# A spectral filter and a two-layer perceptron on one core: the scheduler at build time replaced by a written order, tiles turned by DMA, bias added in place

## The chip, the core and the metric

The kernel runs on one core of a Trainium2 chip. The core has five instruction streams: TensorE (PE; its weight loads are PEld), VectorE (DVE), ScalarE (ACT), GpSimd (POOL) and SyncE (SP, which only issues transfers and waits). Each works through its own list in order, and semaphores order one against another. The metric is device microseconds of one execution, the median of several runs.

## What is computed

All arrays are bf16. `x` has 2048 rows of 640. Each row is normalized, and three terms are added:

```
def reference(A_x, A_w_r, A_w_i, B_x, B_w1, B_b1, B_w2, B_b2):
    x = A_x
    xn = _layernorm(x, axis=-1)
    return x + _A_ref(xn, A_w_r, A_w_i) + _B_ref(xn, B_w1, B_b1, B_w2, B_b2)
```

`_A_ref` is a two-dimensional real FFT, a product with a complex filter of 2048 x 321, and the inverse. `_B_ref` is `gelu(xn @ w1 + b1) @ w2 + b2` with w1 of 640 x 1536 and w2 of 1536 x 640.

## The kernel before

The 2048 rows are 16 tiles of 128. Work goes through these stages.

- *Loads.* SyncE issues the tiles of x, the weights, tables of cosines and sines, the bias row spread over the partitions (`b2bc`, L529), and the filter in 34 loads (`load_w`, L534; 17 real, 17 imaginary). The first third of the first weights goes out on ScalarE's queue (L514).
- *Normalization.* VectorE takes the statistics of a tile in two halves (L568, L570, L572), GpSimd raises the variance to -1/2 (L573), VectorE normalizes (L591).
- *Transposed tile for the perceptron.* TensorE turns each normalized tile in five products with an identity (L608, weights and products), and VectorE or ScalarE copies them out of PSUM into `xnT` (L481, L480).
- *Spectral, forward.* VectorE folds each pair of normalized tiles in six instructions (L620, L624), TensorE multiplies them with the table `gtab` (products "G"), the result goes to `XV`. Then the width stage forward (`etab`, six groups), small 32 x 32 products (`mtab`), the product with the filter on VectorE (L725, L729), small inverse products (`ntab`), copies to U, and sixteen transposing transfers of U to `XV`, issued by SyncE (L750). The width stage back (`getab`, six groups) reads all sixteen.
- *Perceptron.* First layer in blocks of 1, 1, 2, 2, 2, 4 and 4 tiles with 12 column chunks each, gelu on ScalarE (L658). Second layer tile by tile, in pieces of three chunks; each chunk is a pair of products of 512 and 128 columns. For the eight tiles of `KEEP` it is done early and kept.
- *End of a tile.* VectorE unfolds the width stage's result (L775, L780), TensorE multiplies it with `htab` on top of the second layer, VectorE adds the rest (L837), and SyncE stores the tile.
- *The rest, x + b2.* A 32-bit tile is set to the bias row (ScalarE, L805) or to the kept second layer plus the bias row (VectorE, L826); then GpSimd issues a transfer that adds the tile of x from HBM to it (L828), sixteen in all. This is the only use of accumulating transfers.

The order of every engine's list comes from a list scheduler that runs at build time: `Sched.schedule` (L194) takes the estimated cost of every operation (`mm_us`, `dve_us`, `act_us`), its priority (`PRIO`), gates such as `CHAIN`, and a due time for the filter (`WLATE`, L384), and places what can start first. `sync` (L293) then derives the semaphore waits. A buffer from a `Pool` is reused only when its earlier users are done; the normalized pair, `xn`, has two.

Of the kernel before, what the change touches and what calls it, by code (L numbers as in the profile page):

```python
# [7 lines left out]
BF = dt.bfloat16  # L8
# [5 lines left out]
D = 640  # L14
# [13 lines left out]
def _tables():  # L28
# [5 lines left out]
    for s2 in range(16):  # L34
        for m1 in range(64):
            qq, lo, n = m1 // 32, m1 // 16 % 2, m1 % 16
            pair, hi = n % 8 // 2 * 2 + n // 8, n % 2
# [44 lines left out]
    T["I"] = np.eye(128)  # L82
# [3 lines left out]
SWITCH = 0.095  # L86
HOLD = 0.1


def mm_us(n):  # L90
    return max(n / 2400.0 + 0.0027, 0.0265)


def dve_us(n, rate=1.0):
    return 0.066 + n / 960.0 / rate


def act_us(n, ptr=0):
    return 0.067 + n / 1200.0 + 0.078 * ptr


def pool_us(n):
    return 0.075 + n / 500.0


class Buf:
    def __init__(self, name, pool=None, size=1, zone=None):
        self.name, self.pool, self.size = name, pool, size
        self.zone = zone
        self.writers, self.readers = [], []  # L110
        self.slot = None
        self.prev = []
        self.left = None


class Pool:
    def __init__(self, n):
        self.free = [0.0] * n
        self.users = [[] for _ in range(n)]
        self.busy = [False] * n  # L120

    def find(self, buf, now):
        size, n = buf.size, len(self.free)
        best = None
        for lo, hi in buf.zone or [(0, n)]:
            for i in range(lo, hi - size + 1, size if size != 3 else 1):
                if any(self.busy[i:i + size]):
                    continue
                t = max(self.free[i:i + size])
                key = (max(t, now), sum(not b for b in self.busy[i & ~1:(i & ~1) + 2]), sum(not b for b in self.busy[i & ~3:(i & ~3) + 4]), t)  # L130
                if best is None or key < best[0]:
                    best = (key, t, i)
            if best is not None and best[1] <= now + 0.05:
                break
        return best and best[1:]

    def take(self, buf, i):
        buf.slot = i
        buf.prev = [u for j in range(i, i + buf.size) for u in self.users[j]]
        for j in range(i, i + buf.size):  # L140
            self.busy[j] = True

    def give(self, buf, t):
        for j in range(buf.slot, buf.slot + buf.size):
            self.busy[j] = False
            self.free[j] = t
            self.users[j] = buf.writers + buf.readers
# [6 lines left out]
LAT = {"pe": 0.2, "dve": 0.125, "act": 0.16, "pool": 0.12}  # L154


class Sched:
    def __init__(self, nc, engines):
        self.nc = nc
        self.ops = []  # L160
        self.engines = engines
        self.order = {e: [] for e in engines}

    def op(self, engs, prio, emit, reads=(), writes=(), after=(), nbytes=0, gate=(), rate=330e3, alts=None, late=0.0):
        o = Op()
        o.name = writes[0].name if writes else ""
        o.engs, o.prio, o.emit = engs, prio, emit
        o.reads, o.writes, o.after, o.gate = list(reads), list(writes), list(after), list(gate)
        o.nbytes, o.rate, o.late = nbytes, rate, late
        o.alts, o.alt = alts, None  # L170
        o.seq = len(self.ops)
        o.eng, o.done, o.inc, o.count, o.sem = None, False, False, None, None
# [8 lines left out]
    def cost(self, o, e):  # L181
        if o.alts is None:
            return dict(o.engs)[e], None, self.mode
        best = None
        for k, segs in enumerate(o.alts):
            m, t = self.mode, 0.0
            for mode, us in segs:
                t += us + (SWITCH if mode != m else 0.0)
                m = mode
            if best is None or t < best[0] - 1e-9:  # L190
                best = (t, k, m)
        return best

    def schedule(self):  # L194
        free = {e: 0.75 for e in self.engines}
        dma_free = 0.0
        self.mode = "128"
        pend = {e: [] for e in self.engines}
        for o in self.ops:
            for b in o.reads + o.writes:  # L200
                if b.pool is not None and b.left is None:
                    b.left = len(b.readers) + len(b.writers)
        waiting = {}
        users = {}
        for o in self.ops:
            pre = set(o.deps) | set(o.gate)
            waiting[o] = len(pre)
            for d in pre:
                users.setdefault(d, []).append(o)

        def avail(o):
            o.ready = max([o.late] + [d.end for d in o.deps] + [d.start for d in o.gate])
            for e, _ in o.engs:
                pend[e].append(o)
        for o in self.ops:
            if not waiting[o]:
                avail(o)
        left = len(self.ops)
        while left:
            best = None  # L220
            for e in self.engines:
                cands = []
                for o in pend[e]:
                    if o.done:
                        continue
                    r = o.ready
                    ok = True
                    held = []
                    for b in o.writes:
                        if b.pool is not None and b.slot is None:  # L230
                            f = b.pool.find(b, max(r, free[e]))
                            if f is None:
                                ok = False
                                break
                            r = max(r, f[0])
                            held += [(b.pool, i) for i in range(f[1], f[1] + b.size)]
                            for p, i in held[-b.size:]:
                                p.busy[i] = True
                    for p, i in held:
                        p.busy[i] = False  # L240
                    t = max(r, free[e])
                    if ok and len(o.engs) > 1:
                        mine = (t + dict(o.engs)[e], self.engines.index(e))
                        ok = all(e2 == e or (max(r, free[e2]) + d2, self.engines.index(e2)) > mine for e2, d2 in o.engs)
                    if ok:
                        cands.append((t, o))
                if not cands:
                    continue
                t0 = min(c[0] for c in cands)
                near = [c for c in cands if c[0] <= t0 + 0.03]  # L250
                if e == "pe" and self.mode != "128":
                    near = [c for c in cands if c[0] <= t0 + HOLD and c[1].alts and c[1].alts[0][0][0] == self.mode] or near
                t, o = min(near, key=lambda c: (-c[1].prio, c[1].seq))
                if best is None or t < best[0]:
                    best = (t, e, o)
            if best is None:
                raise RuntimeError("nothing can be scheduled: " + str([(e, [p.name for p in pend[e] if not p.done][:5]) for e in self.engines]))
            t, e, o = best
            if e == "pe":
                dur, o.alt, self.mode = self.cost(o, e)  # L260
            else:
                dur = dict(o.engs)[e]
            o.eng, o.start = e, t
            o.done = True
            pend[e] = [p for p in pend[e] if not p.done]
            free[e] = t + dur
            if o.nbytes:
                if e == "pool" and o.prio < 400:
                    o.end = t + 5.0
                else:  # L270
                    s = max(t + 1.1, dma_free)
                    dma_free = s + o.nbytes / o.rate
                    o.end = dma_free + 0.9
            else:
                o.end = t + dur + LAT[e]
            for b in o.writes:
                if b.pool is not None and b.slot is None:
                    b.pool.take(b, b.pool.find(b, t)[1])
# [595 lines left out]
```

## Time and profile before

| | us |
|---|---|
| runs | 157.84, 159.59, 160.26 |
| median | 159.59 |
| span of the profiled execution | 158.2 |
| TensorE busy | 148.9 |
| VectorE busy | 115.0 |
| ScalarE busy | 79.9 |
| GpSimd busy | 26.4 |

The profiled execution is known by its span, from the first to the last instruction; the median of the runs is 1.4 us above it. The span is read in stretches: 0 to 7 us, loads and the first normalization; to 51 us, normalization, transposes, first transform and first layers; to 106 us, filter stages between blocks of the perceptron; to 118 us, the last transposing transfers; to 158 us, width stage back, second layers and stores. A busy TensorE is not TensorE at its pace, since the durations of its products overlap; the pace is the distance from one start to the next.

### The profile page before, as it was taken

The numbers are of one execution on the slowest core, as the hardware profiler recorded it, in microseconds if no ns is written. First come the engines' busy times: TensorE is split into PE (matmuls) and PEld (weight loads), VectorE is DVE, ScalarE is ACT, GpSimd is POOL, SyncE is SP. The second block draws the span as 40 slices with busy tenths as digits, with TensorE's granted clock in tenths as the row PEclk, the third lists the DMA queues.
The fourth block names the chain that finished last, engine by engine and source line by source line (L and its number), as shares of the span: only waits on it lengthen the run. The fifth ranks groups of instructions, "written<-read, shape, count | busy, mean of one in ns | idle before, by whom it ended". The sixth has DMA issues, their size and how long they took to land.

```text
span 158.2 us, 4332 instructions
## 1 busy us (share of the span) xinstructions
PE 148.9 (94%) x1845; PEld 97.1 (61%) x1845; DVE 115.0 (73%) x251; ACT 79.9 (51%) x145; POOL 26.4 (17%) x33
## 2 busy tenths in 40 slices
PE   7699999999999999999999999999749899999993
PEld 7599899989766545445644444454336565665563
DVE  1689999999996448969676969913207999998222
ACT  3178989798984646638563564742402550220000
POOL 1112113233241302000920020022540000000000
PEclk9999999999999999999999999999978999999999
DMA  5999999979853504000799155386992204122111
GB/s 146 358 412 401 395 375 189 206 147 174 147 91 83 77 10 84 3 6 16 125 186 178 41 110 101 55 172 108 156 228 35 83 4 178 73 87 83 41 66 58
DMA packets 30410, 21.71 MB, mean 137 GB/s; under 512 B 12728, under 2 KB 28216, under 8 KB 30392
## 3 DMA queue, kind: packets, MB, share of 16 engines
q1 hardware_dynamic: 23336, 15.71, 37.8%
q0 software_dynamic: 6400, 5.24, 20.4%
q10 hardware_dynamic: 656, 0.49, 0.9%
q8 instruction: 14, 0.23, 0.6%
q14 instruction: 4, 0.03, 0.1%
HBM read 13.58 MB, written 2.62 MB: 102 GB/s over the span
## 4 chain that ended last, share of the span: by engine, by line
PE 80%; DMA 6%; DVE 5%; SPq 3%; ACT 3%; issue 1%; DVEq 0%; POOL 0%
PE ps L469 77%; DMA XV<-U 3%; SPq L750 3%; PE ps L608 3%; DMA X<-in_A_x_dram 2%; DVE T L725 2%; ACT Wf L480 1%; ACT XV L480 1%; DVE Xb L481 1%; DVE Wf L481 1%; DVE Z L729 1%; SPq L464 1%; ACT T L480 0%; DVEq L354 0%; POOL rstd L573 0%
## 5 line engine op out<-in xcount | busy, mean ns | idle before, releaser
L469 PE MATMUL ps<-W,gT 128*128 128x512 bf16 (+3 forms) x396 | 58.6, 298 | 0.5 <-DVE X L826 0.5
L469 PE MATMUL ps<-xnT,W 128*128 128x256 bf16 (+2 forms) x420 | 57.0, 288 | 0.2 <-ACT gT L658 0.2
L469 PEld LDWEIGHTS ps<-W,gT 128*128 128x128 bf16 x396 | 30.4, 99 | 25.1 <-issue 3.2
L658 ACT ACTIVATE gT<-ps,b1col 128x256 bf16<-128x256 f32 (+2 forms) x84 | 39.2, 504 | 10.8 <-PE ps L469 9.5
L469 PEld LDWEIGHTS ps<-xnT,W 128*128 128x128 bf16 x420 | 34.6, 98 | 15.3 <-issue 1.7
L480 ACT ACTIVATE Wf<-ps 128x960 bf16<-128x960 f32 (+1 forms) x9 | 7.6, 880 | 21.1 <-PE ps L469 21.1
L568 DVE BATCH_NORM_STATS2 stats<-X 128x6 f32<-128x320 bf16 x32 | 14.9, 474 | 3.4 <-DMA X<-in_A_x_dram 3.4
L828 POOL DMA_DIRECT2D xnT<-in_A_x_dram x8 | 12.9, 1694 | 24.2 <-ACT xnT L805 20.6
L828 POOL DMA_DIRECT2D X<-in_A_x_dram x8 | 7.4, 923 | 38.4 <-DVE X L826 36.3
L725 DVE TENSOR_TENSOR T<-Y,Wf 128x1288 bf16<-128x1288 bf16 x16 | 12.5, 822 | 0.6 <-issue 0.6
L469 PE MATMUL ps<-getab,XV 32*128 32x160 bf16 (+1 forms) x128 | 8.2, 253 | 3.2 <-DMA XV<-U 2.5
L573 POOL TENSOR_TENSOR rstd<-ve,mhalf 128x2 f32<-128x2 f32 (+1 forms) x9 | 6.4, 716 | 27.1 <-DVE ve L572 27.1
L481 DVE CAST Y<-ps 128x644 bf16<-128x644 f32 x8 | 6.6, 825 | 5.4 <-PE ps L469 5.4
L837 DVE TENSOR_TENSOR W<-ps,xnT 128x640 bf16<-128x640 f32 x8 | 6.5, 819 | 5.6 <-PE ps L469 5.4
L480 ACT ACTIVATE Xb<-ps 128x960 bf16<-128x960 f32 (+1 forms) x6 | 6.8, 1135 | 6.7 <-PE ps L469 6.7
L469 PEld LDWEIGHTS ps<-getab,XV 32*128 32x128 bf16 (+1 forms) x128 | 6.8, 147 | 5.0 <-DMA XV<-U 2.9
L481 DVE CAST Xb<-ps 128x960 bf16<-128x960 f32 (+1 forms) x6 | 6.7, 1122 | 4.2 <-PE ps L469 4.2
L480 ACT ACTIVATE Y<-ps 128x644 bf16<-128x644 f32 x8 | 5.6, 706 | 8.1 <-PE ps L469 8.1
L480 ACT ACTIVATE XV<-ps 128x1280 bf16<-128x1280 f32 (+1 forms) x7 | 8.0, 1145 | 3.4 <-PE ps L469 3.4
L826 DVE TENSOR_TENSOR X<-ps,b2bc 128x640 f32<-128x640 f32 x7 | 5.7, 818 | 4.8 <-PE ps L469 4.8
L624 DVE TENSOR_TENSOR T<-T 128x512 bf16<-128x512 bf16 (+1 forms) x32 | 8.7, 316 | 0.0
L608 PE MATMUL ps<-ident,T 128*128 128x128 bf16 x80 | 7.1, 220 | 1.3 <-DVE T L591 1.3
(46 smaller groups left out, 142.1 us busy)
## 6 DMA issues: line engine op xcount, KB each, us to landing
xnT<-in_A_x_dram POOLq DMA_DIRECT2D x8, 320.0 KB, 5.6
X<-in_A_x_dram POOLq DMA_DIRECT2D x8, 320.0 KB, 4.5
out_dram<-W SPq DMA_DIRECT2D x15, 160.0 KB, 1.8
X<-in_A_x_dram SPq DMA_DIRECT2D x7, 320.0 KB, 9.0
W<-in_B_w_dram SPq DMA_DIRECT2D x2, 960.0 KB, 12.9
Wf<-in_A_w_r_dram SPq DMA_DIRECT2D x15, 80.2 KB, 7.2
Wf<-in_A_w_i_dram SPq DMA_DIRECT2D x15, 80.2 KB, 3.8
W<-in_B_w_dram SPq DMA_DIRECT2D x1, 800.0 KB, 7.3
```

The source lines that it names most:

```text
L469: ins = e.matmul(o_, lhsT=lw, rhs=rh, start=st, stop=sp_, skip_group_check=True)
L480: return e.activation(dst(), src(), ACT.Copy, scale=scale)
L481: return e.tensor_copy(dst(), src())
L568: st_ops.append(K.op([("dve", 0.393)], pr, lambda e, _, c=c, h=h: e.bn_stats(stats[:, c, 6 * h:6 * h + 6], view(X, c * D + H2 * h, [[1, H2 ...
L573: K.op([("pool", 0.65)], pr, lambda e, _, a=a, b=b: e.tensor_tensor(out=rstd[:, a:b], in0=ve[:, a:b], in1=mhalf[:, a:b], op=ALU.pow), read ...
L608: ins = e.transpose(psb(tps.slot, [[1, 512]]).bitcast(BF)[:, 128 * j:128 * j + 128], xnv(n, 128 * j, [[1, 128]]), ident[:])
L624: ring_ops.append(K.op([("dve", dve_us(4 * w, 2))], pr, lambda e, _, op=op, x1v=x1v, xfv=xfv, o_=o_, o0=o0, o1=o1, w=w: e.tensor_tensor(ou ...
L658: K.op([("act", act_us(128 * nt, 1))], pr + PRIO["gelu"], lambda e, _, c0=c0, nt=nt, fc=fc, hps=hps: e.activation(gT[:, fc, 128 * c0:128 * ...
L725: filt_ops.append(K.op([("dve", dve_us(4 * KP, 2))], pr, lambda e, _, k=k, Y=Y, TB=TB, pair=pair: e.tensor_tensor(out=view(TT, TB.slot * 8 ...
L826: kept_ops.append(K.op([("dve", dve_us(D))], 30, lambda e, _, kps=kps, xov=xov, shaped=shaped: e.tensor_tensor(out=xov(0, D), in0=shaped(p ...
L828: K.op([("pool", 1.5)], 51, lambda e, _, c=c, xov=xov, shaped=shaped: e.dma_start(xov(0, D), shaped(xv[:, c, :]), accum_op=ALU.add), reads ...
L837: K.op([("dve", dve_us(w))], 95, lambda e, _, os_=os_, fps=fps, o0=o0, w=w, xov=xov, shaped=shaped, base=base: e.tensor_tensor(out=shaped( ...
```

## The change

`Sched`, its costs, priorities and gates are gone. `Plan` takes the order of all 775 operations and the place of every pooled buffer from two strings, `ORDER` and `SLOTS`, and derives the waits as before. One line of `ORDER` holds operations of several engines; each engine takes its own in the order in which they stand. Beside the order, the work itself is changed in these places:

- Tiles 4 to 15 are turned by a transposing transfer from SyncE (`td`); tiles 0 to 3 stay on TensorE (`tp`, copies `tc`).
- The bias row is added to x in SBUF, in bf16, by four accumulating transfers of four tiles each (`xs0`, `xs4`, `xs8`, `xs12`), issued by GpSimd after the normalizations of those tiles. The 32-bit tiles set on ScalarE and the sixteen transfers of x go. The early sum of a kept tile (`kk`) adds its second layer to x + b2; the last addition (`os`) of the other tiles reads x + b2.
- The filter comes in 18 loads of up to 16 x 16 rows that share a semaphore; the rows of the first transform's table are placed to suit.
- The identity is made on GpSimd. The first weights are loaded on SyncE's queue behind four tiles of x; only the bias of the first layer stays on ScalarE's.
- Weights of the second layer, tables and filter are issued after the last x has landed.
- The two halves of the second weights are waited for separately.
- The block ends without a GpSimd drain, and SyncE waits for the stores behind the block.

```diff
+BYDMA = tuple(range(4, 16))
+SUMS = [(c, c + 4) for c in range(0, 16, 4)]
...
+        for a, b in SUMS:
+            bs = K.buf(f"xs{a}")
+            K.op(f"xs{a}", "pool", lambda e, _, a=a, b=b: e.dma_start(
+                view(X, a * D, [[D, b - a], [1, D]]), view(b2bc, 0, [[0, b - a], [1, D]]), accum_op=ALU.add),
+                reads=[B_b2b] + B_x[a:b], writes=[bs], after=norm_ops[a:b], dma=f"xs{a}")
...
+                    K.op(f"kk{c}", "dve", lambda e, _, kps=kps, c=c, home=home: e.tensor_tensor(
+                        out=home, in0=shaped(psb(kps.slot, [[1, D]])), in1=shaped(view(X, D * c, [[1, D]])), op=ALU.add),
...
-                K.op([("pool", 1.5)], 51, lambda e, _, c=c, xov=xov, shaped=shaped: e.dma_start(xov(0, D), shaped(xv[:, c, :]), accum_op=ALU.add),
-                     reads=[xb2], writes=[xo], nbytes=327680, rate=150e3)
...
         for ri, wsrc in enumerate((A_w_r, A_w_i)):
...
+            for b in range(4):
+                off = ri * KP
+                load_w(f"W{ri}{b}p", wsrc, 32 * b, off, 16 * b, 16, 1)
+                if b:
+                    load_w(f"W{ri}{b}n", wsrc, 32 * b + 1, off, 128 - 16 * b, 16, -1)
+                else:
+                    load_w(f"W{ri}{b}m", wsrc, 1, off, 64, 1, 1)
+                    load_w(f"W{ri}{b}n", wsrc, 1, off + 2 * KP, 127, 15, -1)
...
-        block = es.enter_context(nc.Block())
+        with nc.Block(no_gpsimd_drain=True) as block:
...
+        for o in last:
+            nc.sync.wait_ge(o.sem, o.count)
```

Three places of `ORDER`: the start, the loads and transposes between tile 11 and the end of SyncE's early list, and the last inverse product (`d3.1`) up to the first group of the width stage back (`e0`). `h1.0.3` is block 1, chunk 0, second part of the first layer; `k` and `l` are second-layer pieces, `ge` a gelu, `W..` a filter load, `vt` a transposing transfer of U, `st`, `ag`, `ve`, `rs`, `nm` the normalization's steps, `f1`, `f2` the folds, `G` the first transform, `b` the width stage forward, `m` the product with the filter.

```
act:bias1 pool:id0 dve:warm0 sp:x0 pool:mhalf pool:xbpad1 pool:id1 pe:idle0 act:table sp:x2 sp:x1 sp:w1_0 sp:w1_1 sp:w1_2 dve:st0.1 sp:x4 dve:st0.0
sp:g pe:b1mm dve:ag0 act:b1cp dve:ve0 dve:st2.1 pool:rs0 dve:st1.1 sp:x6 dve:st1.0 pool:xbpad0 dve:nm0 sp:x14 dve:ag1 dve:st2.0 pe:tp0.3 sp:x12
pe:tp0.0 pe:idle1 act:tc0.3 dve:ve1 dve:st3.0 sp:x10 pool:rs1 dve:tc0.0 sp:x8 dve:st3.1 pe:h0.2.0 pe:h0.1.0 dve:nm1 pe:h0.4.0 dve:ag3 pe:h0.4.3
...
pool:xs8 sp:td11 dve:f15.1 dve:f15.0 pe:G8 dve:kk1 pe:G9 pe:k2.9 act:gx4.0 dve:f25.10 dve:f25.00 pe:h3.1.0 sp:td10 dve:f25.11 pe:h3.0.0 dve:f25.01
...
pe:h4.2.0 dve:f27.10 pe:h4.7.0 pe:h4.2.3 pe:G14 act:ge4.2 pe:h4.7.3 sp:i pe:G15 act:ge4.7 pe:h4.8.0 sp:W12p dve:gx7.2 act:gx7.0 pe:h4.8.3 pe:h4.9.0
sp:W11n act:ge4.8 pe:h4.6.0 act:ge4.5 pe:b0 sp:W10n sp:W10p pe:h4.11.0 act:xb0.0 dve:xb0.1 pe:h4.10.0 sp:W03p pe:h4.10.3 pe:h4.6.3 sp:td15 pe:b1
act:ge4.6 act:ge4.10 sp:W13p pe:h5.0.0 act:xb1.1 sp:td14 pe:h5.0.3 act:xb1.0 pe:h4.11.3 pe:h4.9.3 pe:h5.2.0 act:ge4.11 pe:c0.0 act:ge4.9 pe:h5.1.0
...
pe:h6.5.0 act:ge6.4 pe:d3.1 pe:h6.6.0 act:u7.1 pe:h6.7.0 act:ge6.2 sp:vt14 pe:h6.6.3 act:u6.1 pe:h6.7.3 act:ge6.6 pe:h6.8.0 sp:vt13 pe:h6.8.3
pe:h6.5.3 act:ge6.8 sp:vt15 pe:h6.10.0 pe:h6.10.3 pe:h6.9.0 sp:vt12 act:ge6.10 pe:h6.9.3 act:ge6.5 pe:h6.11.0 act:ge6.7 pe:h6.11.3 pe:l0.0.0
act:ge6.11 act:ge6.9 pe:e0 pe:l0.0.3 act:yo0.0 dve:yo0.1 pe:l0.0.6 dve:y20.1 dve:y20.0 pe:e1 dve:yf0.1 dve:yf0.0 pe:fin1.0 dve:yo1.1 act:yo1.0
```

More of the change, by code (lines that the diff above doesn't have):

```diff
@@ L116, with __init__ @@
 class Pool:
-    def __init__(self, n):
-        self.free = [0.0] * n
+    def __init__(self, name, n):
+        self.name = name
         self.users = [[] for _ in range(n)]
[L120 to L147, printed above, removed]
 class Op:
     pass
-LAT = {"pe": 0.2, "dve": 0.125, "act": 0.16, "pool": 0.12}
-class Sched:
-    def __init__(self, nc, engines):
+class Plan:
+    engines = ("sp", "pe", "act", "dve", "pool")
+    def __init__(self, nc):
@@ L159, in __init__ @@
         self.nc = nc
[L160 to L164, printed above, removed]
-        o = Op()
[L166 to L170, printed above, removed]
+        self.ops, self.bufs = [], []
@@ L179, in op, with place @@
         return o
[L181 to L200, printed above, removed]
+    def place(self, order, slots):
+        self.order = {e: [] for e in self.engines}
+        byname = {o.name: o for o in self.ops}
+        homes = dict(slots)
+        for b in self.bufs:
+            if b.pool is not None:
+                b.slot = homes[b.name]
+        done = set()
+        for i, (e, name) in enumerate(order):
+            o = byname[name]
+            assert e in o.engs and all(d in done for d in o.deps), (e, name)
+            o.eng, o.at = e, i
+            for b in o.writes:
@@ L215, in schedule @@
[L215 to L278, printed above, removed]
@@ L299, in sync @@
         know = {e: {} for e in self.engines}
-        final = {}
-        n = len(self.ops)
-        while len(issued) < n:
+        for o in self.ops:
+            o.waits = [d for d in set(o.deps) if d.dma or d.eng != o.eng or o.eng != "pe"]
+        while len(issued) < len(self.ops):
             moved = False
```

577 lines of the change are left out of this document (285 added, 292 removed).

## The prediction

> **What bounds the kernel now.** First the page's head, then two stretches of the busy time by windows (length, then busy time of PE, PEld, DVE, ACT, POOL with instruction counts, granted clock, DMA share, GB/s).
>
> ```profile
> span 158.2 us, 4332 instructions
> ```
>
> ```profile
> 7.18:50.90 43.72, 43.51 (x514) 37.51 (x515) 41.53 (x132) 36.32 (x77) 11.48 (x12) 1.00 0.93 243
> ...
> 106.20:118.00 11.80, 8.79 (x62) 4.69 (x65) 2.50 (x4) 3.39 (x6) 4.75 (x4) 0.94 1.01 164
> ```
>
> TensorE is full in the first stretch (43.5 of 43.7 us), and VectorE nearly so (41.5). In the later one 3.0 of 11.8 us are idle. So time is won by less matmul work, by a shorter hole, or by an earlier start, and VectorE decides whether less matmul work becomes time in the first stretch. The chain that ended last, in order of time, gives TensorE's pace and the hole:
>
> ```profile
> 25.52 0.28 PE ps L608 x5
> 25.80 4.91 PE ps L469 x45
> ...
> 106.31 0.77 ACT T L480 x2
> ...
> 111.69 4.98 DMA XV<-U
> ```
>
> Pace is the distance between starts: five transposes in 0.28 us, 0.056 each, as for any product of 128 columns; 0.109 for 256. The last inverse product ends at 106.2, its copies at 107.1, four transposing transfers go out one after another, the last lands at 116.7, and the stage that reads all sixteen starts.
>
> **The change, part by part.** *Transposes.* Twelve of sixteen input tiles leave TensorE: 12 x 0.28 = **-3.4 us**, on the path because TensorE is full there. VectorE loses twelve copies of the second group, 5.7 us, and gets two early sums of kept tiles.
>
> ```profile
> L608 PE MATMUL ps<-ident,T 128*128 128x128 bf16 x80 | 7.1, 220 | 1.3 <-DVE T L591 1.3
> ...
> L481 DVE COPY xnT<-ps 128x640 bf16<-128x640 bf16 x13 | 6.2, 478 | 0.0
> ```
>
> The row's 220 ns is a duration, and durations overlap: the sum goes by the pace. The page "TensorE: Matmul & The Clock Gate" of the Trainium skill (Part 4, PE-mode transpose) gives some 275 ns for one inside a kernel; taken as a price, 60 of them would be worth 16.5 us. The trace disagrees with that use of it by its five starts in 0.28 us.
>
> *The hole.* The new order puts 32 products of 512 columns of the last first-layer block and three pairs (512 + 128 columns) of the second layer between the last inverse product and the stage that waits. Pace from the kernel's end, 24 products or 12 pairs in 3.26 us: 0.27 a pair, 0.216 for 512 columns:
>
> ```profile
> 148.53 3.42 PE L469 MATMUL ps<-W,gT 128*128 128x512 bf16 x24
> 151.79 0.43 PE L469 MATMUL ps<-Wf,htab 128*128 128x512 bf16 x2
> ```
>
> The cover is 32 x 0.216 + 3 x 0.27 = 7.7 us. The transfers' issue (ns, min/median/max) and landing (median us):
>
> ```profile
> L750 SPq DMA_TRANSPOSE XV<-U x8: 1203/1298/2084, 73.6 to 111.7; - x8
> L750 SPq DMA_TRANSPOSE XV<-gtab x4: 1275/1327/2172, 76.2 to 104.0; - x4
> ```
>
> ```profile
> XV<-U SPq DMA_TRANSPOSE x8, 2.5
> ...
> XV<-gtab SPq DMA_TRANSPOSE x4, 4.7
> ```
>
> Undisturbed the last lands 0.9 (copies) + 3 x 1.3 + 2.5 = 7.3 us after the last inverse product. Before it took 10.4, beside accumulating transfers that GpSimd issued just then and that the change moves to the first third:
>
> ```profile
> 108.28 0.86 POOL L828 DMA_DIRECT2D X<-in_A_x_dram  x1 [4.49 <-DVE X L826]
> 112.63 0.86 POOL L828 DMA_DIRECT2D X<-in_A_x_dram  x1 [3.50 <-DVE X L826]
> 113.55 3.03 POOL L828 DMA_DIRECT2D xnT<-in_A_x_dram  x2
> ```
>
> So 7.3 is covered by 7.7 and the 3.0 us of idle time go. Behind the hole the granted clock was low (PE's windows; the third is the same kind of work as the first, later):
>
> ```profile
> 116.72:118.36 1.64, 1.64 (x17) 0.50 1.41 209
> 118.36:120.82 2.46, 2.46 (x17) 0.65 0.56 83
> 140.23:141.18 0.95, 0.95 (x18) 1.00 0.47 173
> ```
>
> 1.64 against 0.95, and six pairs and the switch in 2.46 against 1.63: 1.5 us that go too. Together **-4.5 us**.
>
> *The loads at the start.* Before, the first third of the first weights came on ScalarE's queue; now every early load stands on SyncE's, four tiles of x ahead of the weights, and the order uses the weights in other places. VectorE stood for tile 1's load ahead of tile 0's variance:
>
> ```profile
> 5.43 0.49 DVE L568 BATCH_NORM_STATS2 stats<-X 128x6 f32<-128x320 bf16 x1 [0.73 <-DMA X<-in_A_x_dram]
> ```
>
> The variance now stands ahead of that: **-0.6**, first products near 7.5 instead of 8.1. When the later loads landed (issue, then time to landing):
>
> ```profile
> L464 SPq DMA_DIRECT2D W<-in_B_w_dram x2: 415/424/434, 2.6 to 3.6; - x2
> ...
> DMA to landing us min/median/max: 5.5/6.4/7.3
> ```
>
> ```profile
> 4.67 0.64 SPq L464 DMA_DIRECT2D gtab<-c_G  x1
> ```
>
> ```profile
> 16.03 0.87 SPq L464 DMA_DIRECT2D b2bc<-in_B_b_dram  x1
> ```
>
> ```profile
> gtab<-c_G SPq DMA_DIRECT2D x1, 512.0 KB, 8.3
> ...
> b2bc<-in_B_b_dram SPq DMA_DIRECT2D x1, 160.0 KB, 8.0
> ```
>
> Second weights at 8.1, third at 10.9, the first transform's table at 13.0. They are bound by bytes, not by issue. Two more tiles of x, 320 KB, stand ahead of the second weights now: 8.8 (an estimate, at the 2.8 us between the second and the third weights' landings for 1.1 MB). The others keep their place. At its pace TensorE wants them at 7.9, 10.7 and 12.1 (35 products of block 0 and a transpose, then 20 more and the first of block 1): waits of 0.9, 0.2 and 0.8, **+1.9**. The old order filled this time with tile 1's products. Then VectorE's pace:
>
> ```profile
> 16.00:50.00 34.00, 32.61 (x105) 1.00 0.92 207
> ```
>
> 0.31 us an instruction. In the new order 57 of them lie between tile 0's normalization (6.0) and the folded tiles that product G5 reads: 17.7, and 0.9 for loads of x: 24.6. TensorE is there after 13.6 us of work from 7.5 and 1.9 of waits: 23.1. **+1.4**, once; afterwards both run level to the first width stage, at 47.5. The old stretch had small waits of its own, 42.8 us from 8.1 to 50.9 for 42.2 of work by the pace, which these replace: -0.6. The start and this stage, beside the transposes: -0.6 + 1.9 + 1.4 - 0.6 = **+2.1**.
>
> *Transposing transfers of the input.* Each frees its half of a two-deep buffer only when landed; the normalization two pairs later waits for it, and VectorE's whole queue behind that. The buffer is wanted some 5.5 us after it was filled; two issues and a landing take 2 x 1.3 + 2.5 = 5.1 undisturbed, 2 x 2.1 + 4.7 = 8.9 disturbed. Of three such pairs: between 0 and about 3 x 3.4 less the slack between VectorE and TensorE, 3 us or so in all. I take **+0.6**, near the undisturbed end, since the group of eight landed in 2.5.
>
> *Accumulating transfers.* Sixteen of one tile become four of four tiles, issued behind four normalizations each; eight copies on ScalarE (half idle) go. Cost 0 if the first has landed when VectorE comes to its first use, 88 instructions behind tile 0's normalization, 6.0 + 27.3 + 0.9, near 34 us. It can go when the bias row is there, at 24.0 before, with the whole second weights ahead of it; now with half of them: I take 21. GpSimd's next power, which VectorE waits for, is queued behind it, but is wanted only near 24.
>
> *Filter loads and SyncE's queue.* 34 loads become 18; twelve transposes join.
>
> ```profile
> 18.37 12.27 SPq L464 DMA_DIRECT2D Wf<-in_A_w_r_dram  x17
> 30.68 11.73 SPq L464 DMA_DIRECT2D Wf<-in_A_w_i_dram  x17
> ```
>
> 0.7 us an issue: 11 us saved, 12 x 1.3 = 16 added, and they wait for VectorE. After tile 10's transpose (35 us) 13 filter loads, 3 transposes and two tables remain: 9.1 + 3.9 + 0.9, last issue at 49, landed by 54; the filter's first product wants it at 56. Cost 0; if an issue took twice as long for twice the rows, see C. The identity built on GpSimd lies under the wait for x. The block's end without a drain: between -0.5 (what lies behind the last landing) and 0; I take 0.
>
> **Sum:** 158.2 - 3.4 - 4.5 + 2.1 + 0.6 = **153.0 us** of span. The median of the runs, 159.6, is 1.4 above this span: **154.4**.
>
> **Rivals.** *A, no new waits:* neither loads nor VectorE hold TensorE in the first stretch. For it: an order written down whole can be laid round landings; against it: the bytes ahead of the table. The +1.9, +1.4 and +0.6 fall away, the small waits stay: 154.4 - 3.9 + 0.6 = 151.1.
> *B, the hole stays:* the cover has 0.4 to spare. With issues of 2.1, the rows' maximum, 9.7 us are needed: 2.0 idle and the 1.5 of low clock come back, 157.9. Against it: no accumulating transfer is near any more.
> *C, the filter late:* if an issue of 256 rows takes 1.4 us, the last load goes at 58 and lands at 62; the inverse product behind it has 1.7 us of slack after 56, so 4.3 us: 158.7. Against it: the weights' 640 rows were issued in 0.43.
> *D, slower: the first accumulating transfer late.* One of one tile landed thus (all sixteen):
>
> ```profile
> DMA to landing us min/median/max: 3.7/5.2/8.9
> ```
>
> If time goes with tiles, 4 x 5.2 = 21: it lands at 42, VectorE stands 8 us in front of its first early sum, TensorE behind it: 162.4. It costs from a landing time of 13 us on, and passes 159.6 at 18. Against it: most of the 5.2 may be fixed, and the written sum is half as wide. The page "SBUF — State Buffer" (the "DVE blocks DMA" trap) says that GpSimd cannot write descriptors while VectorE holds the shared port in its fast modes, which would delay just these. The trace bears it out little: in VectorE's fullest time an issue took 1.66, against 1.5 each at 113.55.
>
> ```profile
> 26.12 1.66 POOL L828 DMA_DIRECT2D xnT<-in_A_x_dram  x1 [2.77 <-ACT xnT L805]
> ```
>
> **How the numbers follow.** Forecast 0.48 (own range 152.4 to 156.6), A 0.20, B 0.12, C 0.11, D 0.09. A difference of 2%, about what a measurement of this kernel can tell from no change, ends at 156.4. Faster: A, nearly all of the forecast, a little of B: 0.69. Same: B, C, the lower half of D and the forecast's upper end: 0.25. Slower, beyond 162.8: the upper half of D and a little else, 0.06. The range 150.6 to 159.2 leaves out D and a part of A.
>
> **What would show it.** Right: four tiles' transposes left on TensorE; the last four transposing transfers issued in 1.3 us each and no wait ahead of the last width stage; TensorE waiting for weights and table between 8 and 13 us; the first width stage near 47.5. Wrong: a chain that ends in the filter's loads near 56 us; VectorE standing at an early sum near 34 us; input transposes that land after 5 us and more with a normalization behind them.

## The result and the profile after

The changed kernel takes 172.57 us (median of four runs, 172.44 to 173.25) against 159.88 (median of four) for the kernel before: 1.086 times the time (1.079 by these medians), 95% interval 1.077 to 1.095. The forecast was 154.4, in a range of 150.6 to 159.2. The runs of some kernels here fall into two groups (the kernel before 2% apart, others up to 6%); ratios compare the faster group, and where a profile is of the other one, this is said.

Head of the page after, with the busy tenths of TensorE and of the DMA engines (40 slices of 4.3 us):

```profile
span 171.3 us, 4167 instructions
...
PE   7789988902999999907998999999989899999995
...
DMA  5999899997999999700072017253600124030204
```

Two holes stand in TensorE's row where before there was one, in other places, and the DMA engines are full or nearly so from 4 to 70 us. The windows put borders on what follows (length; busy time of PE, PEld, DVE, ACT, POOL; granted clock; DMA share; GB/s). The first width stage starts at 58.63, the last at 124.87.

```profile
8.81:33.94 25.13, 22.92 (x275) 18.77 (x277) 22.97 (x78) 17.75 (x42) 6.75 (x8) 1.00 1.04 286
33.94:41.58 7.64, 0.22 (x2) 0.01 (x1) 0.96 (x4) 0.00 (x0) 0.00 (x0) 0.87 1.29 174
41.58:58.63 17.05, 17.05 (x152) 14.12 (x153) 12.47 (x33) 10.91 (x23) 4.20 (x4) 0.86 1.15 164
58.63:72.70 14.07, 13.20 (x205) 7.36 (x207) 2.54 (x3) 10.56 (x15) 0.00 (x0) 1.00 1.07 163
72.70:77.94 5.24, 0.35 (x2) 0.00 (x0) 4.74 (x8) 1.86 (x3) 0.00 (x0) 0.92 0.00 0
77.94:84.00 6.06, 5.73 (x89) 1.75 (x106) 3.20 (x6) 2.05 (x4) 0.00 (x0) 0.51 0.01 3
84.00:124.87 40.87, 39.05 (x587) 19.27 (x567) 23.30 (x39) 26.69 (x48) 0.00 (x0) 1.00 0.40 66
124.87:171.30 46.43, 43.21 (x413) 27.87 (x420) 29.49 (x46) 8.59 (x11) 0.00 (x0) 1.00 0.16 58
```

In each hole the timeline shows TensorE behind VectorE, and VectorE behind a transposing transfer of the input. First TensorE's two rows, then VectorE's:

```profile
41.58 1.25 PE L400 MATMUL ps<-gtab,T 128*128 128x128 bf16 x10 [7.42 <-DVE T L542]
...
77.94 0.77 PE L400 MATMUL ps<-Xb,mtab 32*32 32x322 bf16 x32 [4.89 <-DVE Y L411]
```

```profile
40.59 0.80 DVE L516 TENSOR_SCALAR T<-X,mv,rstd 128x640 bf16<-128x640 bf16 x2 [7.99 <-DMA xnT<-T]
```

```profile
73.17 3.04 DVE L638 TENSOR_TENSOR T<-Y,Wf 128x1288 bf16<-128x1288 bf16 x4 [5.66 <-DMA xnT<-T]
```

L516 at 40.59 is the normalization of tile 10, into the buffer from which tiles 6 and 7 are still being transferred (issued at 26.64 and 28.19, landed at 39.98 and 40.50). L638 at 73.17 is the first product with the filter. It writes over the buffers of the normalized tiles, so it waits for the last input transpose (tile 14, issued at 64.47, landed at 73.09). After each hole TensorE is slow: 17.05 us at a clock of 0.86 and 6.06 at 0.51. By an estimate, which takes TensorE to be what these stretches wait for, that cost 17.05 x 0.14 + 6.06 x 0.49 = 5.4 us beside the 7.4 + 4.9 idle: 17.7 in all. The chain of waits in order of time says the same:

```profile
28.19 12.31 DMA xnT<-T
40.59 0.80 DVE T L516 x2
...
64.47 8.62 DMA xnT<-T
73.17 3.06 DVE T L638 x4
```

The transfers, medians from issue to landing in us, and min/median/max of the transposes of the input:

```profile
X<-b2bc POOLq DMA_DIRECT2D x4, 640.0 KB, 10.5
...
xnT<-T SPq DMA_TRANSPOSE x12, 7.8
```

```profile
DMA to landing us min/median/max: 2.7/7.8/13.3
```

What the two kinds do to each other stands in the DMA view of a window, queue by queue. From 34 to 36 us an accumulating transfer (q0) and transposes (q1, 256 bytes a packet) are in flight together; from 40 to 41 the transposes are alone:

```profile
q0 software_dynamic: 215, 0.28, 82.6%
q1 hardware_dynamic: 221, 0.06, 26.4%
```

```profile
q1 hardware_dynamic: 1082, 0.27, 128.0%
```

221 packets in two microseconds beside 215 of the other queue, 1082 in one microsecond without it: the transposes run at a tenth of their rate. (ScalarE's queue moved 135 small packets in the same two microseconds.) An accumulating packet (1280 bytes) takes 120 ns, a transposing one 18 when alone.

One packet against one is not all of it. From 28 to 30 us both tiles had been issued, and not one packet of 256 bytes moved:

```profile
DMA packets 321, 0.40 MB, mean 199 GB/s; under 512 B 0, under 2 KB 321, under 8 KB 321
...
q0 software_dynamic: 300, 0.38, 113.4%
q1 hardware_dynamic: 21, 0.01, 3.0%
```

Tiles 6 and 7 stood on SyncE's own queue behind a filter load and the table `htab` (512 KB, issued at 25.33, landed 8.5 us later), and these moved 21 packets against 300 accumulating ones. The first packets of the two tiles moved between 32 and 33 us, some six us after tile 6 was issued; the turns of one against one came after that. Why 300 stood against 21 stays open.

The Trainium skill, page "DMA: Bandwidth & Descriptors", section "Queues, rings and completion order", says that each DMA engine takes turns between the queues that have work for it, a packet at a time. 215 against 221 fits that, 300 against 21 does not fit equal turns; and since the page counts typically 9 to 17 descriptors to a packet, its packet need not be one of the profile's.

### The profile page after: what moved, and what is told of

It is laid out like the page before. It is cut to its first block, busy times and chain, and to the rows that moved or that the text cites. A ratio compares the mean times of both kernels' runs of the same rounds, so it can differ in the third digit from the quotient of the medians.

```text
span 171.3 us, 4167 instructions
## 1 busy us (share of the span) xinstructions
PE 148.3 (87%) x1777; PEld 95.4 (56%) x1798; DVE 104.0 (61%) x229; ACT 80.3 (47%) x147; POOL 13.0 (8%) x23
## 3 DMA queue, kind: packets, MB, share of 16 engines
q1 hardware_dynamic: 31488, 18.09, 48.5%
## 4 chain that ended last, share of the span: by engine, by line
PE 41%; DMA 24%; SPq 14%; DVE 13%; ACT 4%; issue 3%; DVEq 0%
PE ps L400 41%; DMA xnT<-T 16%; SPq L395 10%; DMA X<-in_A_x_dram 5%; DVE stats L494 3%; SPq L520 3%; ACT Xb L410 2%; DVE T L638 2%; ACT gT L582 2%; DMA XV<-T 2%; DMA out_dram<-W 1%; DVE T L516 1%; DVE T L538 1%; DVE W L733 1%; DVE Y L411 1%
## 5 line engine op out<-in xcount | busy, mean ns | idle before, releaser
L400 PE MATMUL ps<-xnT,W 128*128 128x256 bf16 (+2 forms) x413 | 59.6, 295 | 2.0 <-issue 1.0
L400 PE MATMUL ps<-W,gT 128*128 128x128 bf16 (+4 forms) x395 | 56.3, 291 | 2.4 <-issue 0.9
L638 DVE TENSOR_TENSOR T<-Y,Wf 128x1288 bf16<-128x1288 bf16 x16 | 12.5, 820 | 5.7 <-DMA xnT<-T 5.7
L400 PE MATMUL ps<-gtab,T 128*128 128x128 bf16 x80 | 7.5, 235 | 7.9 <-DVE T L542 7.9
L410 ACT ACTIVATE Xb<-ps 128x960 bf16<-128x960 f32 (+1 forms) x10 | 10.9, 1151 | 3.8 <-PE ps L400 3.8
L516 DVE TENSOR_SCALAR T<-X,mv,rstd 128x640 bf16<-128x640 bf16 x16 | 6.6, 440 | 9.5 <-DMA xnT<-T 8.0
L400 PEld LDWEIGHTS ps<-gtab,T 128*128 128x128 bf16 x80 | 6.0, 107 | 8.9 <-DVE T L542 8.5
L722 DVE TENSOR_TENSOR xnT<-ps,X 128x640 f32<-128x640 f32 x8 | 6.6, 821 | 5.8 <-PE ps L400 5.8
L733 DVE TENSOR_TENSOR W<-ps,X 128x640 bf16<-128x640 f32 (+2 forms) x10 | 6.9, 688 | 5.1 <-PE ps L400 5.1
L400 PE MATMUL ps<-Xb,mtab 32*32 32x322 bf16 x256 | 4.2, 321 | 5.6 <-DVE Y L411 4.9
L695 DVE TENSOR_TENSOR Wf<-Wf 128x960 bf16<-128x960 bf16 (+1 forms) x12 | 7.0, 596 | 2.6 <-ACT Wf L410 2.4
```

The costliest lines, as they stand in the source:

```text
L400: ins = e.matmul(o_, lhsT=lw, rhs=rh, start=st, stop=sp_, skip_group_check=True)
L410: return e.activation(dst(), src(), ACT.Copy)
L516: norm_ops.append(K.op(f"nm{c}", "dve", lambda e, _, c=c, n=n, xnv=xnv: e.tensor_scalar(out=xnv(n, 0, [[1, D]]), in0=view(X, c * D, [[1, D ...
L638: filt_ops.append(K.op(f"m{pair}.{k}", "dve", lambda e, _, k=k, Y=Y, TB=TB, pair=pair: e.tensor_tensor(out=view(TT, TB.slot * 8 * KP + k * ...
L695: K.op(f"y2{gi}.{k}", "dve", lambda e, _, k=k, op=op, yo=yo, y2=y2, n=n: e.tensor_tensor(out=view(Wf, Y2 + y2.slot * 3 * D + (H2 - 1) * k, ...
L722: K.op(f"kk{c}", "dve", lambda e, _, kps=kps, c=c, home=home: e.tensor_tensor(out=home, in0=shaped(psb(kps.slot, [[1, D]])), in1=shaped(vi ...
```

## The experiments

Theory H2: the accumulating transfers hold the input transposes, packet for packet; these hold the buffers, VectorE, and TensorE in turn. H1: the transposes stand behind filter loads on SyncE's ring. H3: so many small packets cost the time whatever is beside them.

**1. No accumulating transfers.** The sums read X as it is.

```diff
-        for a, b in SUMS:
-            bs = K.buf(f"xs{a}")
-            K.op(f"xs{a}", "pool", ...
+        B_xs.update({c: B_x[c] for c in range(16)})
```

> The changed kernel without its four accumulating transfers: the bias row is left out of the output, X is read as it is. Theory H2 (the accumulating transfers, packet for packet beside the input transposes, hold the buffers of normalized tiles, VectorE and then TensorE): the transposes of tiles 6 and 7 land within 5 us of their issue instead of 12 to 13, the 7.4 us idle time of TensorE at 34 us shrinks below 1 us, the first width stage starts near 49, the time is 153 to 160. H1 (the transposes stand behind filter loads on SyncE's ring) and H3 (too many small packets in all): tiles 6 and 7 still take over 9 us, and the time stays above 168.

Measured 155.5 us (154.8 to 156.2), 0.979 of the time before (0.944 to 1.015). The stretches of the profiled run (span 153.5):

```profile
8.50:48.60 40.10, 37.75 (x429) 31.32 (x428) 35.62 (x113) 28.61 (x65) 5.43 (x8) 1.00 1.06 240
48.60:107.23 58.63, 57.48 (x878) 28.03 (x877) 33.63 (x55) 41.08 (x70) 0.00 (x0) 1.00 0.46 71
107.23:153.50 46.27, 43.91 (x420) 27.90 (x420) 29.50 (x46) 8.60 (x11) 0.00 (x0) 1.00 0.16 58
```

```profile
xnT<-T SPq DMA_TRANSPOSE x12, 4.8
```

The first width stage comes 10.0 us sooner than in the changed kernel, the stretch to the last one is 58.6 instead of 66.2, the rest is the same: 10.0 + 7.6 + 0.2 = 17.8, the whole difference of the spans. The clock is 1.00 throughout. H3 falls: the twelve transposes are all still there. So are the loads ahead of them on SyncE's queue, so these alone don't make the transposes late either.

**2. The transposes alone, in the kernel before.** The old planner supports it.

```diff
-BYDMA = ()
+BYDMA = tuple(range(4, 16))
```

> The kernel before, whose scheduler places twelve input transposes on the DMA queues (tiles 4 to 15) and leaves all else as it was: accumulating transfers of one tile that come late, filter in 34 loads. H3 (the transposes by DMA cost the time whatever stands beside them): 165 to 175. H2: nothing accumulates beside them, so no long stall from this, 155 to 161. H1: its filter loads are issued early, by 42 us, so transposes stand among them: stalls of 2 to 5 us in the first stretch, 160 to 166.

167.5 us in the faster run (the profile is of one of 170.6). The time lies in the range of H3 and outside those of H2 and H1, but not for H3's reason: the transposes land in 4.0 us (median), and the first width stage starts at 48.2, sooner than before (50.9). The loss is behind it: the filter's first product waits 5.1 us for filter loads, which stand behind the transposes on SyncE's queue, and the planner's order is another one from there on. How the loss divides between the two was not measured. Inconclusive for H2.

**3. Filter loads on another queue.**

```diff
-            load(name, "sp", bass.AP(tensor=Wf, ...
+            load(name, "act", bass.AP(tensor=Wf, ...
```

> The changed kernel with its eighteen filter loads issued on ScalarE's queue at the same places of the order, so that no input transpose stands behind one on SyncE's ring. H1: tiles 12 to 15 land 3 to 4 us after their issue instead of 8 to 9, the 4.9 us stall of TensorE at 73 us goes, and the time falls to 160 to 165 (ScalarE pays 18 issues of 0.6 us, of which it has the time). H2: the stall at 34 us stays (tiles 6 and 7 were issued ahead of nearly all filter loads); the one at 73 us shrinks at most by half, 167 to 171. H3: no change, 170 to 174.

172.5 us in the faster run: no gain, and above what I expected under H2 too. In the profile (of a run of 175.6) the transposes take longer than before, not shorter:

```profile
DMA to landing us min/median/max: 2.6/8.5/15.2
```

H1 falls for the filter loads: freed from their place behind them, the transposes share the engines with them. From 62 to 63 us of this run 87 accumulating packets, 82 of SyncE's queue and 83 of ScalarE's moved. The table `htab` stayed ahead of tiles 6 and 7 on SyncE's queue, so what its place costs beside an accumulating transfer was not tested. The same page of the Trainium skill says, in "Rules for kernel authors", that spreading transfers over the issuing engines doesn't help, since they interleave on the same DMA engines; this run agrees.

**4. Accumulating transfers held back.** Those of tiles 4 to 15 wait for all twelve transposes; the first stays.

```diff
-                reads=[B_b2b] + B_x[a:b], writes=[bs], after=norm_ops[a:b], ...
+                reads=[B_b2b] + B_x[a:b], writes=[bs], after=norm_ops[a:b] + ring_ops * (a > 0), ...
```

> The changed kernel with three of its four accumulating transfers (tiles 4 to 15) held until all twelve input transposes have landed; the first one stays. Nothing is left out. H2: the stall at 34 us shrinks from 7.4 to 2 to 4 us (the first transfer still runs beside the transposes of tiles 4 to 7), and the time falls to 160 to 167; new cost if the late transfers run beside the inverse transposes or late sums. H1 and H3: 171 to 176.

158.1 us (eight runs), 1.001 of the time before (0.995 to 1.008), better than the 160 to 167 expected: 14.5 of the 17.1 us come back with nothing left out.

```profile
8.50:51.82 43.32, 38.43 (x430) 31.26 (x430) 36.24 (x114) 28.64 (x65) 6.90 (x9) 1.00 1.09 245
51.82:110.81 58.99, 57.47 (x877) 28.02 (x877) 33.78 (x55) 41.21 (x70) 3.93 (x3) 1.00 0.69 103
```

The one transfer left beside the loads and early transposes costs 3.2 us (43.3 against 40.1); the three later ones, 1.9 MB from 61 to 75 us, cost 0.4.

**5. The other two corners.** All sixteen tiles on TensorE, with the accumulating transfers and without; the plan chooses the places of the new PSUM buffers.

```diff
-BYDMA = tuple(range(4, 16))
+BYDMA = ()
-... sp:td5 ...
+... pe:tp5.0 dve:tc5.0 ...
```

> The changed kernel with all sixteen input tiles turned by TensorE (five transposes and a copy by VectorE or ScalarE where the transposing transfer stood), its four accumulating transfers as they are. If the loss is the meeting of the two kinds of transfer, taking away the one is worth as much as taking away the other: no stall of VectorE before a normalization, the time is that of the run without accumulating transfers (155.5) plus 3.4 for the transposes: 156 to 161. If the accumulating transfers cost time by themselves (port, late first sum, late filter), it stays above 165.

> The changed kernel with all sixteen input tiles turned by TensorE and without the accumulating transfers (the bias row is left out of the output): the fourth corner beside the changed kernel (172.6), the one without accumulating transfers (155.5) and the one without transposing transfers of the input (162.5). If the loss is the meeting of the two kinds of transfer: the accumulating transfers cost little here, 158 to 160, and the twelve transposes on TensorE cost 3.4 against the 155.5. If they cost as much with nothing beside them, 145 to 150.

| | accumulating transfers | none |
|---|---|---|
| twelve tiles turned by DMA | 172.6 | 155.5 |
| all on TensorE | 162.5 | 162.1 |

The accumulating transfers cost 0.4 us without input transposes and 17.1 with them; 16.7 us are the meeting. Both new runs lie above what I expected, by 1.5 and 2 us: the transposing transfers save 6.6, not 3.4. In the first stretch TensorE is busy for 40.75 us instead of 37.75, so 3.0 of it are the transposes; the other 3.3 are idle time, probably since the order was not made for sixteen tiles on TensorE:

```profile
8.50:54.85 46.35, 40.75 (x472) 33.71 (x474) 37.55 (x116) 31.67 (x70) 5.42 (x8) 1.00 0.84 199
```

The busy tenths of the DMA engines on the pages give another account of the meeting. The kernel before, and the run without accumulating transfers (experiment 1):

```profile
DMA  5999999979853504000799155386992204122111
```

```profile
DMA  4999889979999990008100662654001240210205
```

All tiles on TensorE, with the accumulating transfers and without:

```profile
DMA  5999699999999920000710054255201222210204
```

```profile
DMA  5999899999910000000810054345201222210204
```

In slices of some 4 us, the engines stay nearly full to about 70 us in the changed kernel and to 57 without accumulating transfers; with all tiles on TensorE, to 57 and 44. In both pairs the accumulating transfers fill some 13 us more. With all tiles on TensorE that ends near the start of the first width stage (55.7), and no product waits for a filter load; with transposes by DMA the last of these lands at 73.1 instead of 58.0, and the filter's first product waits for it. By their share of the span (9.9% of 171.3) the accumulating packets took some 17 us of all sixteen engines, an estimate since packets of one engine overlap. So the sum of the engines' time fits the size of the loss as well as turns do, and no experiment separates the two.

**6. One transfer or four.** Sixteen of one tile, issued at the same places.

```diff
-SUMS = [(c, c + 4) for c in range(0, 16, 4)]
+SUMS = [(c, c + 1) for c in range(16)]
```

> The changed kernel with its four accumulating transfers of four tiles cut into sixteen of one tile, issued at the same places one behind the other; nothing left out. If the packets and their place decide, not the size of a transfer: 169 to 175, tiles 6 and 7 landing after 10 us and more. If it was the size of the transfer: below 165.

167.1 us in the faster run, 171.7 in the other. 167.1 is below the 169 to 175 and above the 165 expected: most of the loss stays with the place of the packets, and by the faster run 5.5 of the 17.1 us go with the grouping. With one run that size is not firm.

**7. Plain copies instead of accumulation**, of the same bytes, from the same places, over free buffers of the filter stage; the same into rows 1288 bytes apart; and sixteen of one tile.

```diff
-                view(X, a * D, [[D, b - a], [1, D]]), view(b2bc, ...), accum_op=ALU.add),
+                view((Yb, Zb)[a // 4 % 2], 0, [[D, b - a], [1, D]]), view(b2bc, ...)),
```

> The changed kernel whose four transfers write the bias row over free buffers of the filter stage instead of adding it to x: same queue, places, sizes and reads, but no accumulation; the bias row is left out of the output. If it is the accumulation that makes a packet slow (some 120 ns for 1280 bytes), the transposes pass beside plain packets and the time falls to 154 to 160, with tiles 6 and 7 landing within 6 us. If any GpSimd transfer of this size, packet for packet, holds them as much, 168 to 173.

> As the run with plain copies instead of accumulation, but into rows 1288 bytes apart, so that each transfer is 512 packets of 1280 bytes, as the accumulating ones are (the plain copies before went in 128 packets of 5120). Bias row left out. If the number of packets on the other queue holds the transposes: 167 to 173, as the changed kernel. If it is how long an accumulating packet takes (120 ns against some 55 of a plain one of 1280 bytes): 158 to 164, as with the long packets.

> The changed kernel with sixteen plain copies of the bias row, one tile each, over free buffers of the filter stage, at the places of the sixteen accumulating transfers; 512 packets of 1280 bytes for each four of them, as there, but without accumulation; the bias row is left out of the output. If the number of packets on the other queue sets how long the transposes take: the same as sixteen accumulating ones, 166 to 172. If a packet's time does (some 55 ns of a plain one of this size against 120): the same as with the plain copies of 5120 bytes or better, 157 to 163.

162.6 (other run 171.9), 162.5 (other 167.5) and 165.6 us (four runs, 164.6 to 167.1). The first lies between the two ranges expected. The question of the last two was not put by them: however they were written, the copies went in packets of 5120 bytes, 512 in all, 230 to 240 ns each (median), while the accumulating ones are 2048 packets of 1280 bytes. The DMA view by queue, changed kernel, then first run of copies:

```profile
q0 software_dynamic: 2112, 2.62, 9.9%
```

```profile
q0 software_dynamic: 576, 2.62, 5.3%
```

So a plain copy of the same bytes takes half the engines' time (5.3% of 161.3 us, some 8.5 by the same estimate), in a quarter of the packets, and still costs 7 to 10 of the 17.1 us; two of the three times rest on one run. That plain copies from GpSimd's queue cost time here too is shown; the loss goes nearer with the engines' time, a half, than with the number of packets, a quarter. How much of the rest is the accumulation and how much the number of packets stays open.

**8. The second hole alone.** Tiles 12 to 15 on TensorE.

```diff
-BYDMA = tuple(range(4, 16))
+BYDMA = tuple(range(4, 12))
```

> The changed kernel with tiles 12 to 15 turned by TensorE; tiles 4 to 11 still by transposing transfers, accumulating transfers as they are. If the second stall (the filter's first product waits for the last input transpose) is a loss of its own of some 7.6 us: the first width stage stays near 58 to 60, the stretch between the first width stage and the last falls from 66.2 to 59 to 60, and the time is 164 to 167. If that product would wait for its filter loads or the last accumulating transfer anyway: 169 to 173.

168.2 us, 1.057 of the time before (1.047 to 1.067); outside the 164 to 167, since the first stretch grew by 1.8. The second hole is a loss of its own: 60.40 from the first width stage to the last, against 66.2.

```profile
60.46:120.86 60.40, 56.83 (x875) 28.54 (x887) 34.11 (x56) 41.56 (x71) 0.00 (x0) 1.00 0.47 77
```

**9. The bias added by an engine.** Sixteen additions by VectorE, or by GpSimd.

```diff
-            K.op(f"xs{a}", "pool", lambda e, _, a=a, b=b: e.dma_start(...
+            K.op(f"xs{c}", "pool dve", lambda e, _, c=c: e.tensor_tensor(
+                out=view(X, c * D, [[1, D]]), in0=view(X, c * D, [[1, D]]), in1=b2bc[:], op=ALU.add),
```

> The changed kernel with the bias row added to x by VectorE (sixteen additions of 128 by 640, some 0.48 us each as the fold's, two of them in the first third, the others from 75 us on where VectorE waits for TensorE) instead of by accumulating transfers; nothing left out. H2: as fast as the run without them plus the two early additions at most, 155 to 157.5, and faster than the kernel before by 1 to 2%. If VectorE has no room for 7.7 us more: 159 to 163.

> The changed kernel with the bias row added to x by GpSimd's own instructions (sixteen additions of 128 by 640: two behind the power of tiles 8 and 9, the others behind the last filter load), no accumulating transfer; nothing left out. If they run beside VectorE without holding it: 154 to 156, as the run without the bias. If they hold VectorE while both use the memory port, or the two early ones delay the next power, which VectorE waits for: 157 to 162.

VectorE: 156.3 us (155.7 to 156.7), 0.989 (0.978 to 1.0005), as expected, though the interval reaches 1. GpSimd: 174.3 us, 1.101 (1.091 to 1.110), far above both ranges expected. My edit did not do what I wrote there: nothing made the fourteen later additions wait, and GpSimd ran them at 41.9 to 62.4, beside VectorE's folds, which became slow. The same group of VectorE's, without the bias and here, and the stretch of the additions:

```profile
L542 DVE TENSOR_TENSOR T<-T 128x128 bf16<-128x128 bf16 x16 | 3.1, 213 | 0.1
```

```profile
L542 DVE TENSOR_TENSOR T<-T 128x128 bf16<-128x128 bf16 x16 | 8.8, 570 | 0.1
```

```profile
41.88:62.40 20.52, 10.37 (x74) 7.96 (x72) 20.42 (x15) 5.66 (x14) 20.52 (x15) 0.83 1.07 158
```

Fifteen instructions of VectorE beside fifteen of GpSimd in 20.5 us: they go by turns. GpSimd's additions behind the folds weren't tried.

**10. The best version.** VectorE adds, but the two early sums get the bias later, in place, and tile 0's normalization stands ahead of tile 1's statistics.

```diff
-... pool:rs0 dve:st1.1 sp:x6 dve:st1.0 pool:xbpad0 dve:nm0 ...
+... pool:rs0 dve:nm0 dve:st1.1 sp:x6 dve:st1.0 pool:xbpad0 ...
-... dve:xs1 dve:kk1 ...
+... dve:kk1 ... dve:u6.0 dve:xs1 dve:xs2 ...
```

> The version with the bias added by VectorE, but nothing of it left in the first third (the two early sums get their bias row later, in place), and with tile 0's normalization ahead of tile 1's statistics. All of the computation is there. 154 to 155.5, as the run without the bias, and 2 to 3% faster than the kernel before; the first width stage near 48.5 instead of 50.4. If the 1.6 us between those two runs were only scatter of the loads: 156 to 157.

155.32 us (six runs, 154.8 to 156.3), 0.976 of the time before (0.970 to 0.982): faster than both kernels by this interval, though not clearly by 2%, and all of it computed. Its slowest run is below the fastest of the eleven runs of the kernel before beside it (157.8). The first width stage starts at 49.07, later than the 48.5 expected: the normalization came sooner, at 5.33 instead of 5.65, but the first products wait for the weights all the same.

## Why the prediction was wrong, step by step

- **Accumulating transfers, "Cost 0 if the first has landed when VectorE comes to its first use": the step that failed.** The condition held: the first was issued at 23.33 and landed at 33.58, and no sum waited for it. But I priced them only by who reads their result. They cost 17.1 us through what is in flight beside them. No term of the sum is the DMA engines' own time, though the prediction's first row has their share at 0.93: by an estimate from that row some 3 of 43.7 us were free, and the accumulating packets took some 17, beside twelve transposes. Rival D had the right suspect and the wrong victim. The rule of the Trainium skill beside it ("SBUF — State Buffer", the "DVE blocks DMA" trap: VectorE keeps GpSimd from writing descriptors) did not show in the issues: the four took 1.3 to 1.5 us. The first one's packets moved only from 27 to 28 us on, some four us after its issue; what held them is not shown.
- **Transposing transfers of the input, "+0.6".** The chain was the right one (a half of a two-deep buffer, the normalization two pairs later, VectorE's whole queue). The size was bounded by 2.5 and 4.7 us, medians of the inverse transposes' landings. The two of the second row that were issued from 76 us on, beside three accumulating transfers of one tile (issued at 75.4 to 77.3), took 5.3 and 8.4. The line for all sixteen, kernel before, reads `DMA to landing us min/median/max: 2.4/3.3/8.4`. So the effect stood in the trace before, and the medians hid it. Here tiles 6 and 7 took 13.3 and 12.3; without the accumulating transfers the median is 4.8, and no normalization waits for a transpose.
- **The filter, "Cost 0": also failed.** The loads were timed and a wait was missed: the filter's first product writes where the normalized tiles lay, so it also waits for the last input transpose, behind filter loads on SyncE's queue. That is the second hole, 4.9 us idle and 3.0 of low clock; 0.6 us on VectorE remain of it when nothing accumulates. Rival C expected the loads themselves late, at 1.4 us for an issue of 256 rows; undisturbed it took 0.6.
- **The clock behind a stall** was priced for the hole that goes (1.5 us) and for no new one: 5.4 us of the 17.7, by the estimate above.
- **The hole, -4.5: right.** The last width stage starts 0.4 us after TensorE is free, and runs at 1.00.
- **Twelve transposes, -3.4: right for TensorE** (3.0 us of its busy time).
- **Start and loads, +2.1: near, in part by luck.** Without the accumulating transfers the first width stage starts at 48.6 (forecast 47.5), since the first product comes at 8.4 instead of 7.5; the weights' waits are 1.5 us, forecast 1.1 for the two. The table's 0.8 and VectorE's 1.4 (by its own numbers 24.6 - 23.0 = 1.6) show in no wait of TensorE in that run; the later start and small waits, 1.0 for gelu among them, fill their place.
- **The sum** without the failed step was 153.0 us of span; the run without accumulating transfers spans 153.5. That they are so near is in part luck: the start and the transposing transfers missed both ways, and that run leaves the bias out.

## What to carry to other kernels

A transfer moved earlier is to be priced by what else is in flight there, not only by when its result is needed: write down for each stretch which queues have packets in the DMA engines, and take a landing time only from a row with the same company. Add up the engines' time there as well; here a stretch with a DMA share near 1 had no room, and what was put in delayed what landed last. Many small packets beside slow ones go at the pace of the slow ones (here 110 a microsecond instead of 1050); place the two in different stretches (experiment 4) or do the slow one on an engine with room (experiment 10). Count as readers of a transfer's source all who will write over it: a buffer that is used again makes a late transfer into a wait far from its own stage.

## What the runs showed of the hardware

- Two queues can go packet by packet although the sizes differ: 215 packets of 1280 bytes against 221 of 256 in two microseconds, which alone go at some 1050 a microsecond (1082 with 32 others). They don't always: 300 accumulating packets went beside 21 of a load from 28 to 30 us.
- On the kernel before, a transpose beside accumulating transfers of one tile landed after 8.4 us, against a median of 3.3.
- An accumulating packet within SBUF takes 120 ns for 1280 bytes; a plain copy takes some 235 for 5120, half the time for the same bytes (9.9% and 5.3% of the engines' span).
- GpSimd's additions with two operands in SBUF and VectorE's folds go by turns, fifteen of each in 20.5 us: an addition takes 1.5 us, and a fold of 128 columns 570 ns on average instead of 213. The page "SBUF — State Buffer" of the Trainium skill ("Who interferes with whom") says that a VectorE instruction with two inputs in SBUF contends with a GpSimd instruction that reads it, and one waits for the other; this run agrees.
